# Splitting weight pieces by two recipes in turn, with the float32 words of all thirds in one place

## The chip, the cores and the metric

The kernel runs on one core of a Trainium2 chip. Its engines are TensorE (PE; its weight loads are shown as PEld), VectorE (DVE), ScalarE (ACT), GpSimd (POOL) and SyncE (SP), which here only issues transfers. The metric is the device time of one execution in microseconds (us); the median of the runs is quoted.

## The reference

Two layers are computed, one after the other, in float32: attention with a compressive memory, and a gated feed-forward layer.

```
# q, k, v: (4, 8, 576, 64); M_prev: (4, 8, 64, 64); z_prev: (4, 8, 64)
scores = q @ k^T / 8, causal;  a = softmax(scores);  local = a @ v
q_p = where(q > 0, q, exp(q) - 1) + 1
mem_out = (q_p @ M_prev) / (q_p @ z_prev + 1e-6)
x = sigmoid(beta) * mem_out + (1 - sigmoid(beta)) * local      # rows: 4*576 = 2304, columns: 8*64 = 512
xn = x / sqrt(mean(x*x) + 1e-6) * rms_g
out = (silu(xn @ w_gate) * (xn @ w_val)) @ w_out               # 512 -> 1536 -> 512
```

The three weight matrices arrive as float64; the host only lays inputs out.

## The kernel before

**Split numbers.** All matrix work runs on pairs of float16 numbers: a float32 operand, scaled by a power of two, is written as hi (its float16 rounding) and lo (what is left, in float16 too), and a product takes three matmuls: hi by hi, hi by lo, lo by hi. Most work of the other engines is making such pairs.

**Blocks.** The 2304 rows are 18 blocks of 128 (four batches of 576 rows, two batches taken together, so that each pair has eight full blocks and one block of two tails). For a block `q_stats`, `prep_q`, `phi_calc`, `prep_phi`, `prep_k` and `prep_v` split the rows of q, phi(q), k and v (tiles `row16`, shown as row; v in `v16`); transposing DMAs on SP's queue make qT, phT and kT of them (`tposed`; the first two blocks use TensorE and evictions by ACT instead). For one or more heads at a time, `u_scores` computes scores (tile sc) and moves them out with the mask on VectorE (L449, tile S), `u_exp` takes the exponential and the hi cast on ACT (L495, L497, tile P16), `u_lo` the lo on VectorE or POOL (L506) with a transposing DMA into PT, and `u_pv` multiplies by v (tile loc). `loc_evac` (L595, L601, L605), `x_norm` and `x_split` make the split x, its transposed form being xT, one for two blocks (a chunk of 256 rows; nine chunks).

**The feed-forward layer.** The 1536 inner columns are twelve groups of 128. For chunk c and group f, F = 12c + f: `m_proj` makes 24 matmuls (L762) into gv (gate and value), `m_act` the tanh on ACT (L768) and two operations on VectorE (L769, L772), `m_split` the hi on ACT (L793) and the lo on POOL (L794), `m_down` six matmuls by w_out (L816 to L818). PSUM has two gv buffers.

**The weights.** Gate and value weights come in 24 pieces of 128 x 512, numbered p = 8t + 4m + cc: t is the third of the inner columns, m is 0 for gate and 1 for value, cc the 128 rows of the model dimension. w_out has 12 pieces. For each piece:

- `load_w`: a 512 KB load of the float64 words into one of five raw places (`RING`), which is free again when the piece five earlier is converted. The first five are issued on SP's queue, the others on ACT's.
- `w_conv`: `f64_to_f32` makes float32 words of it with one operation on ACT (L687) and two on VectorE (L691 on the raw words, L692 on the result); `gram` adds their squares up on TensorE (csum, L135).
- `gv_scales(t)`, when all eight pieces of a third are there: reduction (L707), scale factors, and at the end `rgs` (L714), the scale of each piece's rows.
- `w_split`: the words become hi and lo in `wgv16`.

`wgv` is one tile of 25 places of 128 x 512 float32. The words of piece p lie in place p + 1; the pair hi, lo of piece p fills place p (`wgv16` is the same tile seen as float16). So hi of piece p overwrites the words of piece p - 1, and must wait until these have been read. `load_pre` borrows eight places of the last third (17 to 24) for early k and v rows, which only `first_gram` reads.

`wo` has the same scheme for w_out (words of piece f in place f + 1, its pair in place f), and its free places serve as raw ring and for other early data.

**`split` and its recipes.** `SPLIT` names the recipe, one string per third and one for w_out; `way_of` takes its characters in turn by the piece's number.

- "0": ACT writes hi from the words with the scale (L82), VectorE writes lo = words x scale - hi (L85).
- "1": ACT scales the words in place (L97), ACT casts hi (L101), POOL writes lo = words - hi (L104).
- "3": VectorE scales the words in place (L99), ACT casts hi (L101), POOL writes lo (L104).

**What sets the order.** The program is written as attention steps interleaved with feed-forward steps by a budget (`run`, `a_until`), the first blocks with a high priority; a scheduler then fixes each engine's order from the dependencies and these priorities before the run. On the chip each engine executes its list in that order, and an instruction that waits holds up all behind it on its engine.

Of the kernel before, what the change touches and what calls it, by code (L numbers as in the profile page):

```python
# [31 lines left out]
A3 = 0.2  # L32
A4 = 0.3
C2 = 8
SPLIT = ("3", "3", "3", "3")
VWAY = "11"
RING = 5
PACE = 5
# [7 lines left out]
def attn_memory_moe_kernel(  # L46
# [18 lines left out]
    NI = S // P  # L65
    TR = S - NI * P
    NC = DM // P
# [21 lines left out]
    def split(dst_hi, dst_lo, src, scale, way="0"):  # L89


        if way == "0":
            hi_cast(dst_hi, src, scale)
            lo_cast(dst_lo, src, scale, dst_hi)
            return
        if way in "12":
            nc.scalar.activation(src, src, AF.Copy, scale=scale)  # L97
        else:
            nc.vector.tensor_scalar(src, src, scale, None, op0=ALU.mult)  # L99
        if way in "135":  # L100
            nc.scalar.copy(dst_hi, src)  # L101
        else:
            nc.vector.tensor_copy(dst_hi, src)
        nc.gpsimd.tensor_tensor(dst_lo, src, dst_hi, ALU.subtract)  # L104
# [23 lines left out]
    def gram(acc, src, first, last):  # L128

        hi = src.bitcast(BF16).rearrange("p (f w) -> p f w", w=2)[:, :, 1]
        for g in range(4):
            w = hi[:, g * P : (g + 1) * P]
            nc.tensor.matmul(acc[:, :P], w, w, start=first and g == 0, stop=last and g == 3)  # L135

    csum = {}
# [24 lines left out]
    wgv = const.tile([P, 2 * NC * NT3 + 1, 512], F32, name="wgv")  # L162
# [73 lines left out]

    def load_pre(n):

        at = 1 + 4 * NC + 2 * (n - NI)
        pre[n] = wgv[:, at : at + 2, :]  # L240
        nc.sync.dma_start(out=pre[n], in_=qkv[n, :, :2, :])

# [390 lines left out]
    def piece(m, cc, t):  # L633
        return t * 2 * NC + m * NC + cc

    raws = {}
    NR = RING

# [7 lines left out]
    def after(ins, before, why):  # L646
        tc.add_manual_dep(
            ins.ins, before.ins.name,
            mybir.DependencyInfo(mybir.DependencyClass.Sync, mybir.DependencyReason.SCHED_ONLY),
            reason=why,  # L650
        )
# [7 lines left out]
    def load_w(m, cc, t):  # L659
        w = (w_gate, w_val)[m]  # L660
        p = piece(m, cc, t)
        raws[p] = hold(p, 2 * (p % NR))
        ins = (nc.sync if p < PACE else nc.scalar).dma_start(
            out=raws[p].bitcast(I64), in_=w[cc * P : (cc + 1) * P, t * 512 : (t + 1) * 512]
        )
        paced(ins, p)
# [12 lines left out]
    def f64_to_f32(raw, dst, p):  # L679

        r = raw.rearrange("p (f w) -> p f w", w=2)
        ri, di = r.bitcast(I32), dst.bitcast(I32)
        begun[p] = nc.scalar.activation(dst, r[:, :, 1], AF.Prelu, scale=2.0 ** -112, alpha=2.0 ** 32)  # L687
        if 2 * NC <= p < 6 * NC:

            after(begun[p], xdone[p // (2 * NC) - 1], "first blocks")  # L690
        nc.vector.tensor_scalar(ri[:, :, 0], ri[:, :, 0], 29, None, op0=ALU.logical_shift_right)  # L691
        nc.vector.scalar_tensor_tensor(  # L692
            out=di, in0=di, scalar=3, in1=ri[:, :, 0], op0=ALU.logical_shift_left, op1=ALU.bitwise_or
        )

    def way_of(table, third, i):
        return table[third][i % len(table[third])]
# [38 lines left out]

    def w_split(m, cc, t):
        p = piece(m, cc, t)
        src = wgv[:, p + 1, :]
        sc = rgs[:, t, m, cc : cc + 1]  # L740
        split(wgv16[:, p, :512], wgv16[:, p, 512:], src, sc, way_of(SPLIT, t, p % (2 * NC)))

    def wo_split(f):
        src = wo[:, f + 1, :]
        split(wo16[:, f, :512], wo16[:, f, 512:], src, wos[:, f // 4 : f // 4 + 1], way_of(SPLIT, NT3, f))

# [170 lines left out]
    for n in range(NI, 2 * NI):  # L917
        load_pre(n)
# [18 lines left out]
    for s in range(len(units) + LAG + 2):  # L937
        if s < len(units):
            n, h = units[s]
# [25 lines left out]
        if s < len(units):  # L965
            n, h = units[s]
# [8 lines left out]
    def w_conv(i):  # L975
        m, cc, t = pcs[i]
        p = piece(m, cc, t)
        f64_to_f32(raws.pop(p), wgv[:, 1 + p, :], i)
        held.pop(p)
        if cc == m == 0:  # L980
            csum[t] = ps.tile([P, 2, P], F32, tag="out", name="csum")
        gram(csum[t][:, m], wgv[:, 1 + p, :], cc == m == 0, cc == NC - 1 and m == 1)
        if i + PACE < len(pcs):
            load_w(*pcs[i + PACE])

# [52 lines left out]
    def conv(t):  # L1038
        return [lambda i=i: w_conv(i) for i, x in enumerate(pcs) if x[2] == t]

    def spl(t):
        return [lambda: gv_scales(t)] + [lambda x=x: w_split(*x) for x in pcs if x[2] == t]
# [96 lines left out]
```

## Time and profile before

| | |
|---|---|
| runs | 685.72, 685.72, 687.58 us; median 685.72 |
| profiled execution | 687.62 us, of which the span of its instructions is 685.9 |
| TensorE busy | 597.1 us (87% of the span), 6292 matmuls |
| VectorE busy | 480.8 us (70%) |
| ACT busy | 406.9 us (59%) |
| POOL busy | 232.3 us (34%) |
| mean granted TensorE clock | 0.938 of full speed |

The profile divides the span into 40 slices of 17 us. TensorE's busy share is 20 to 80% up to about 180 us and 90% or more in nearly all slices after that; the granted clock is at full speed from about 200 us on and lower in several slices before. VectorE is at 70% or more in every slice from 34 to 154 us. An idle stretch of an engine is shown with the engine or transfer that ended it (its releaser); an operation's duration includes the time in which it is held up after its start.

### The profile page before, as it was taken

How to read it: one execution, taken by the hardware profiler on the slowest of the kernel's cores; microseconds unless marked ns; L12 is line 12 of the kernel's file. 1: busy time of each engine (PE TensorE's matmuls, PEld its weight loads, DVE VectorE, ACT ScalarE, POOL GpSimd, SP SyncE). 2: the span in 40 equal slices, each digit the busy share in tenths (PEclk: the TensorE clock that was granted, in tenths of full speed). 3: DMA queues.
4: the chain of work that ended last, by engine and by line, in shares of the span. 5: the costliest groups of instructions: out<-in, count | busy, mean ns of one | idle time of the engine just before them, and what ended most of it. 6: DMA issues, size and time to landing. Idle time of an engine off the chain costs nothing.

```text
span 685.9 us, 16422 instructions
## 1 busy us (share of the span) xinstructions
PE 597.1 (87%) x6292; PEld 461.3 (67%) x6292; DVE 480.8 (70%) x1441; ACT 406.9 (59%) x845; POOL 232.3 (34%) x308
## 2 busy tenths in 40 slices
PE   2664367866899999999899999999999999999997
PEld 1553245745665587778678777767777878887774
DVE  3689997985685766679687776786887686873221
ACT  5788655665647676657556657766666464442322
POOL 1306544674467434323025231431322222212111
PEclk9985567977899999999999999999999999999999
DMA  8952589833935968844675865376664554441001
GB/s 271 411 148 83 188 272 227 184 77 80 176 69 89 191 126 166 166 88 88 118 155 123 167 131 113 64 137 142 123 131 103 107 78 93 80 76 34 32 1 31
DMA packets 186383, 88.13 MB, mean 128 GB/s; under 512 B 171712, under 2 KB 171712, under 8 KB 186304
## 3 DMA queue, kind: packets, MB, share of 16 engines
q1 hardware_dynamic: 181392, 70.81, 49.5%
q10 hardware_dynamic: 4912, 16.28, 7.1%
q8 instruction: 49, 0.80, 0.5%
q14 instruction: 30, 0.25, 0.1%
HBM read 36.20 MB, written 4.72 MB: 60 GB/s over the span
## 4 chain that ended last, share of the span: by engine, by line
PE 43%; DVE 17%; DMA 16%; ACT 13%; issue 5%; POOL 4%; SPq 1%; ACTq 0%; DVEq 0%; POOLq 0%
PE gv L762 23%; DMA kv<-in_qkv_dram 6%; DMA PT<-P 5%; PE out L816 4%; PE out L817 4%; PE out L818 4%; DVE S L449 3%; ACT junk L220 2%; PE sc L443 2%; DMA qT<-row 2%; ACT P L497 2%; PE sc L469 2%; ACT S L495 2%; DVE P L506 2%; DMA phT<-row 2%
## 5 line engine op out<-in xcount | busy, mean ns | idle before, releaser
L762 PE MATMUL gv<-xT,wgv 128*128 128x256 f16 x2592 | 363.4, 279 | 11.7 <-DVE th L772 6.4
L762 PEld LDWEIGHTS <-wgv 128*128 128x128 f16 x2592 | 253.2, 100 | 56.0 <-issue 7.6
L794 POOL TENSOR_TENSOR h<-th,h 128x256 f16<-128x256 f32 x96 | 71.5, 745 | 259.3 <-ACT h L793 201.2
L495 ACT ACTIVATE S<-S,nm 128x128 f32<-128x128 f32 (+4 forms) x144 | 80.2, 586 | 57.3 <-DVE nm L456 42.2
L443 PE MATMUL sc<-kT,qT 128*128 128x128 f16 x640 | 94.9, 224 | 12.9 <-DMA kT<-row 4.1
L506 DVE TENSOR_TENSOR P<-S,P 128x512 f16<-128x512 f32 (+2 forms) x80 | 61.0, 763 | 40.4 <-ACT P L497 39.7
L769 DVE SCALAR_TENSOR_TENSOR th<-th,gv 128x256 f32<-128x256 f32 x108 | 44.9, 416 | 61.0 <-ACT th L768 60.6
L768 ACT ACTIVATE th<-gv,wt 128x256 f32<-128x256 f32 x108 | 50.4, 467 | 59.4 <-PE gv L762 56.2
L449 DVE CUSTOM_DVE_ANT_0 S<-sc,mask,qsc 128x128 f32<-128x128 f32 (+3 forms) x128 | 66.6, 545 | 12.6 <-PE sc L443 12.0
L817 PE MATMUL out<-wo,h 128*128 128x512 f16 x192 | 72.8, 379 | 0.0
L816 PE MATMUL out<-wo,h 128*128 128x512 f16 x192 | 72.6, 379 | 0.1
L818 PE MATMUL out<-wo,h 128*128 128x512 f16 x192 | 71.8, 379 | 0.0
L443 PEld LDWEIGHTS <-qT 128*128 128x128 f16 x640 | 56.6, 100 | 21.9 <-issue 8.0
L497 ACT CAST P<-S 128x512 f16<-128x512 f32 (+2 forms) x104 | 62.2, 599 | 10.2 <-DMA PT<-P 9.0
L793 ACT CAST h<-th 128x256 f16<-128x256 f32 x96 | 38.5, 402 | 44.7 <-DVE th L772 44.2
L530 PE MATMUL loc<-v,PT 128*128 128x65 f16 x320 | 55.4, 197 | 5.7 <-DMA PT<-P 5.3
L532 PE MATMUL loc<-v,PT 128*128 128x65 f16 x320 | 54.9, 197 | 2.0 <-ACT PT L347 2.0
L531 PE MATMUL loc<-v,PT 128*128 128x64 f16 x320 | 54.9, 197 | 0.0
L772 DVE SCALAR_TENSOR_TENSOR th<-th,wt,gv 128x256 f32<-128x256 f32 x108 | 51.6, 478 | 1.9
L605 POOL TENSOR_TENSOR t<-t,t 128x256 f32<-128x256 f32 x36 | 31.4, 873 | 60.0 <-DVE t L601 57.7
L530 PEld LDWEIGHTS <-PT 128*128 128x128 f16 x320 | 31.6, 100 | 14.2 <-DMA PT<-P 10.8
L104 POOL TENSOR_TENSOR wgv<-wgv 128x512 f16<-128x512 f32 x24 | 31.7, 1321 | 26.8 <-ACT wgv L101 26.6
(222 smaller groups left out, 1104.4 us busy)
## 6 DMA issues: line engine op xcount, KB each, us to landing
kv<-in_qkv_dram SPq DMA_DIRECT2D x18, 512.0 KB, 4.8
wo<-in_moe_w_val_dram ACTq DMA_DIRECT2D x11, 512.0 KB, 4.7
q<-in_qkv_dram SPq DMA_DIRECT2D x18, 256.0 KB, 3.5
wo<-in_moe_w_gate_dram ACTq DMA_DIRECT2D x8, 512.0 KB, 6.0
wo<-in_moe_w_out_dram ACTq DMA_DIRECT2D x8, 512.0 KB, 5.1
qT<-qT SPq DMA_DIRECT2D x32, 128.0 KB, 2.6
out_dram<-res SPq DMA_DIRECT2D x16, 256.0 KB, 2.3
wo<-in_moe_w_gate_dram SPq DMA_DIRECT2D x4, 512.0 KB, 6.5
```

Source lines behind the costliest of these rows:

```text
L443: nc.tensor.matmul(t[:, g * w + j * P : g * w + (j + 1) * P], qT[n][:, t2, h, :], kT[blk_of[(b, j)]][:, h, :], start=(t2 == 0), stop=(t2 = ...
L449: nc.vector.tensor_tensor_reduce(out=s[:, g * w : (g + 1) * w], in0=t[:, g * w : (g + 1) * w], in1=mask[:, m0 : m0 + w], scale=qsc[n][:, 5:6],
L495: nc.scalar.activation(v_, v_, AF.Exp, bias=nm[:, g : g + 1], scale=-1.0)
L497: nc.scalar.copy(p16[:, : G * w], s[:, : G * w])
L506: eng.tensor_tensor(p16[:, w : 2 * w], s[:, :w], p16[:, :w], ALU.subtract)
L530: nc.tensor.matmul(a, phi_, vhi, start=(j == 0), stop=False)
L531: nc.tensor.matmul(a[:, :D], phi_, vlo, start=False, stop=False)
L762: nc.tensor.matmul(o, lhs, xT[c][:, rhs, :], start=(cnt == 0), stop=(cnt == 3 * NC - 1))
L794: nc.gpsimd.tensor_tensor(h16[:, 1], th, h16[:, 0], ALU.subtract)
L816: nc.tensor.matmul(o, hh, whi, start=(f == 0), stop=False)
L817: nc.tensor.matmul(o, hh, wlo, start=False, stop=False)
L818: nc.tensor.matmul(o, hl, whi, start=False, stop=(f == NF - 1))
```

## The change

`SPLIT` is "01" in all four entries: of each third, and of w_out, the pieces with an even number are split by recipe 0 (hi on ACT, lo on VectorE), those with an odd number by recipe 1 (two operations on ACT, lo on POOL). The words of piece p now lie in place 17 + p mod 8 for all three thirds, and `load_pre` borrows places 9 to 16. So the words of a third overwrite those of the third before, whose split must have read them; the pairs of the first two thirds no longer overwrite words. In the last third, words and pairs lie as before.

```
-SPLIT = ("3", "3", "3", "3")
+SPLIT = ("01", "01", "01", "01")
...
     def load_pre(n):
-        at = 1 + 4 * NC + 2 * (n - NI)
+        at = 1 + 2 * NC + 2 * (n - NI)
...
+    def words_at(p):
+        return 1 + 4 * NC + p % (2 * NC)
...
     def w_split(m, cc, t):
         p = piece(m, cc, t)
-        src = wgv[:, p + 1, :]
+        src = wgv[:, words_at(p), :]
...
     def w_conv(i):
-        f64_to_f32(raws.pop(p), wgv[:, 1 + p, :], i)
+        f64_to_f32(raws.pop(p), wgv[:, words_at(p), :], i)
-        gram(csum[t][:, m], wgv[:, 1 + p, :], cc == m == 0, cc == NC - 1 and m == 1)
+        gram(csum[t][:, m], wgv[:, words_at(p), :], cc == m == 0, cc == NC - 1 and m == 1)
```

NC is 4 and NI is 4. Because of four added lines, lines from 636 on have numbers higher by four in the changed kernel (L687 becomes L691, L663 becomes L667, L676 becomes L680, L768 becomes L772, L692 becomes L696).

The scheduler's order changes with it. On ACT, around the split of the first third, before the change (x is the split x of block 0, kv the rows of v being scaled, xT evictions and v casts follow):

```order
L82 ACTIVATE x_713<-t_0_580,xs 128x512
L101 CAST wgv<-wgv 128x512
L97 ACTIVATE kv_117<-kv_117,cb_92 128x512
L97 ACTIVATE kv_119<-kv_119,cb_92 128x512
L97 ACTIVATE kv_921<-kv_921,cb_92 128x512
L97 ACTIVATE kv_501<-kv_501,cb_92 128x512
L687 ACTIVATE wgv<-wo 128x512 x5
L347 CAST xT_716<-tp 128x4x128
```

and after it, from the same instruction on (the two operations on wgv stand there four times in turn, for the eight pieces; L691 is the word conversion):

```order
L82 ACTIVATE wgv<-wgv,rgs 128x512
L97 ACTIVATE wgv<-wgv,rgs 128x512
...
L97 ACTIVATE kv_117<-kv_117,cb_92 128x512
L97 ACTIVATE kv_119<-kv_119,cb_92 128x512
L97 ACTIVATE kv_917<-kv_917,cb_92 128x512
L97 ACTIVATE kv_501<-kv_501,cb_92 128x512
L82 ACTIVATE x_711<-t_0_580,xs 128x512
L101 CAST wgv<-wgv 128x512
L97 ACTIVATE kv_125<-kv_125,tcb_898 128x512
L101 CAST wgv<-wgv 128x512 x3
L101 CAST v_2_1089<-kv_117 128x8x64
```

The x cast has moved behind the split, and the five conversions of the middle third behind both.

On VectorE at the same place, before the change (fl and t belong to the attention output, ratio, kT and v to a rescaling of the first blocks):

```order
L99 TENSOR_SCALAR wgv<-wgv,rgs 128x512 x5
L291 TENSOR_TENSOR ratio<-cb_92,wo 128x4
L598 RECIPROCAL fl<-fl 128x4
L85 SCALAR_TENSOR_TENSOR x_713<-t_0_580,xs,x_713 128x512
L721 TENSOR_SCALAR wt<-wt 128x1
L302 TENSOR_SCALAR kT_192<-kT_192,ratio 128x1024
L304 TENSOR_SCALAR v_0_268<-v_0_268,ratio 128x1040
L302 TENSOR_SCALAR kT_473<-kT_473,ratio 128x1024
L601 TENSOR_TENSOR t_1_792<-loc_0_779,fl 128x256
L692 SCALAR_TENSOR_TENSOR wgv<-wgv,wo 128x512 x5
```

and after it:

```order
L291 TENSOR_TENSOR ratio<-cb_92,wo 128x4
L598 RECIPROCAL fl<-fl 128x4
L725 TENSOR_SCALAR wt<-wt 128x1
L85 SCALAR_TENSOR_TENSOR wgv<-wgv,rgs 128x512
L302 TENSOR_SCALAR kT_192<-kT_192,ratio 128x1024
L304 TENSOR_SCALAR v_0_268<-v_0_268,ratio 128x1040
L302 TENSOR_SCALAR kT_473<-kT_473,ratio 128x1024
L601 TENSOR_TENSOR t_1_788<-loc_0_775,fl 128x256
L85 SCALAR_TENSOR_TENSOR wgv<-wgv,rgs 128x512 x3
L85 SCALAR_TENSOR_TENSOR x_711<-t_0_580,xs,x_711 128x512
L696 SCALAR_TENSOR_TENSOR wgv<-wgv,wo 128x512 x5
```

Eight scalings are gone (three more stand just ahead of the first list), four lo's have come, and the lo of x stands behind them.

On ACT some 40 us later, before the change from the gate tanh of F = 1 (gv_984) on, with the first loads of w_out:

```order
L768 ACTIVATE th<-gv_984,wt 128x256
L101 CAST wgv<-wgv 128x512
L676 DMA wo<-in_moe_w_out_dram 128x512
L676 DMA rawo_1815<-in_moe_w_out_dram 128x512
L97 ACTIVATE kv_1101<-kv_1101,cb_92 128x512
L395 ACTIVATE ph<-q_1099 128x512
```

and after it, at the first loads of w_out (row_1172 and row_1305 are the rows of q and k of block 3, gv_1074 is F = 2):

```order
L82 ACTIVATE row_1172<-q_1094,qsc 128x8x64
L691 ACTIVATE wgv<-wo 128x512
L667 DMA wo<-in_moe_w_val_dram 128x512
L82 ACTIVATE row_1305<-kv_119,cb_92 128x8x64
L797 CAST h16k<-th 128x256
L691 ACTIVATE wgv<-wo 128x512
L772 ACTIVATE th<-gv_1074,wt 128x256
L691 ACTIVATE wgv<-wo 128x512
L667 DMA wo<-in_moe_w_val_dram 128x512
L680 DMA wo<-in_moe_w_out_dram 128x512 x2
```

The loads of w_out have moved behind loads and conversions of the last third's value pieces, and behind the rows of block 3.

## Rows read from the trace of the kernel before

**Rows 1.** Stretches of the span: length, busy us of each engine, clock, DMA, GB/s.
```profile
55.50:151.00 95.50, 59.09 (x536) 45.45 (x536) 87.92 (x228) 62.15 (x121) 55.60 (x51) 0.69 0.69 182
...
180.00:686.00 506.00, 488.81 (x5287) 378.54 (x5285) 340.79 (x1017) 290.17 (x607) 151.70 (x205) 1.00 0.53 106
...
200.00:236.00 36.00, 32.64 (x307) 20.74 (x306) 22.85 (x74) 25.60 (x54) 23.75 (x27) 1.00 0.64 119
```
**Rows 2.** Groups by line, 55.5 to 151 us: count, busy us, mean ns, idle before.
```profile
L104 POOL TENSOR_TENSOR wgv<-wgv 128x512 f16<-128x512 f32 x20 | 27.1, 1354 | 24.7 <-ACT wgv L101 24.5
...
L99 DVE TENSOR_SCALAR wgv<-wgv,rgs 128x512 f32<-128x512 f32 x24 | 14.1, 640 | 0.0
L691 DVE TENSOR_SCALAR wo<-wo 128x512 int32<-128x512 int32 x19 | 13.5, 723 | 1.3 <-DMA wo<-in_moe_w_val_dram 1.3
L101 ACT CAST wgv<-wgv 128x512 f16<-128x512 f32 x21 | 12.9, 614 | 5.3 <-POOL wgv L104 5.3
```
**Rows 3.** Single lines over the whole span: ns min/median/max, first and last start.
```profile
L99 DVE TENSOR_SCALAR wgv<-wgv,rgs x24: 452/476/1382, 55.5 to 139.7; 128x512 f32<-128x512 f32 x24
...
L691 DVE TENSOR_SCALAR wo<-wo x32: 405/421/1381, 13.4 to 123.8; 128x512 int32<-128x512 int32 x32
...
L85 DVE SCALAR_TENSOR_TENSOR row<-q,qsc,row x18: 740/752/1647, 25.2 to 527.0; 128x512 f16<-128x512 f32 x18
...
L85 DVE SCALAR_TENSOR_TENSOR row<-kv,cb,row x14: 735/744/752, 91.6 to 522.1; 128x512 f16<-128x512 f32 x14
```
**Rows 4.** Whom VectorE waited for, 55.5 to 151 us: total, times, longest.
```profile
DVE row L85 <- ACT row L82: 4.1, 1, 4.1
```
**Rows 5.** Transfers of phT, 80 to 115 us and whole run: count, us to landing.
```profile
phT<-row SPq DMA_TRANSPOSE x1, 10.9
...
phT<-row SPq DMA_TRANSPOSE x16, 2.8
```
**Rows 6.** ACT in order of time: start, us, line, operation, count, idle before.
```profile
55.99 0.72 ACT L82 ACTIVATE x<-t,xs 128x512 f16<-128x512 f32 x1 [1.02 <-POOL xs L618]
...
57.12 2.56 ACT L97 ACTIVATE kv<-kv,cb 128x512 f32<-128x512 f32 x4
59.59 2.88 ACT L687 ACTIVATE wgv<-wo 128x512 f32<-128x512 f32 x5
...
63.27 0.33 ACTq L663 DMA_DIRECT2D wo<-in_moe_w_val_dram  x1
...
97.41 0.33 ACTq L676 DMA_DIRECT2D wo<-in_moe_w_out_dram  x1
...
109.65 0.72 ACT L82 ACTIVATE row<-q,qsc 128x512 f16<-128x512 f32 x1 [5.51 <-DMA phT<-row]
```
**Rows 7.** VectorE in order of time, columns as in rows 6.
```profile
55.12 0.22 DVE L714 TENSOR_SCALAR rgs<-rg,wt 128x4 f32<-128x4 f32 x1
...
66.98 0.61 DVE L691 TENSOR_SCALAR wo<-wo 128x512 int32<-128x512 int32 x1 [1.34 <-DMA wo<-in_moe_w_val_dram]
...
72.43 0.15 DVE L595 SCALAR_TENSOR_TENSOR fl<-loc,wo 128x4 f32<-128x4 f32 x1
...
80.71 0.74 DVE L85 SCALAR_TENSOR_TENSOR x<-t,xs,x 128x512 f16<-128x512 f32 x1
...
90.00 1.65 DVE L85 SCALAR_TENSOR_TENSOR row<-q,qsc,row 128x512 f16<-128x512 f32 x1
...
99.23 0.42 DVE L707 TENSOR_REDUCE wmx<-csum 128x2 f32<-128x256 f32 x1
...
132.63 0.77 DVE L714 TENSOR_SCALAR rgs<-rg,wt 128x4 f32<-128x4 f32 x2
```
**Rows 8.** POOL and TensorE in order of time; ACT's waits in 136 to 162 us.
```profile
89.61 1.49 POOL L104 TENSOR_TENSOR wgv<-wgv 128x512 f16<-128x512 f32 x1 [3.37 <-ACT wgv L101]
...
163.74 6.37 PE L762 MATMUL gv<-xT,wgv 128*128 128x256 f16 x44 [2.22 <-DVE th L772]
...
ACT wgv L101 <- POOL wgv L104: 4.6, 3, 2.6
```

## The prediction

> **What bounds the kernel now.** I read the stages first [rows 1]. From 180 us to the end TensorE is busy for 488.8 of 506.0 us at full clock: there the end is set by how much matrix work is left, and only an earlier arrival at that state saves time. Before it TensorE mostly starves: in 55.5 to 151.0 it is busy 59.1 of 95.5 us at a mean granted clock of 0.69, a mixture of 1.2 and 2.4 GHz. In the same stretch VectorE is busy 87.9 of 95.5 us, ACT 62.2 and POOL 55.6. VectorE therefore bounds 55.5 to 151, the stretch in which all 24 VectorE scalings of gate and val pieces and 20 of the 24 POOL subtracts lie [rows 2]. Of its 7.6 idle us, 4.1 are one wait for ACT [rows 4], which itself waits 5.51 us for the transposing DMA of phT [rows 6]. From 151 to 164 the bound is a chain: TensorE waits for the last third's splits and for the gate arithmetic behind them, and goes on at 163.74 [rows 8]. The wo pieces lie in 200 to 236, where TensorE is busy 32.6 of 36.0 us, so their edits are nearly covered.
>
> **Against which time.** The profiled execution took 687.62 us (span 685.9 plus 1.7 around it); the median of the three runs is 685.72, 1.9 lower. I sum differences against the profiled one and set them off from the median.
>
> **The change, part by part.** Prices of the added operations stand in rows of the same shapes: a scaled hi cast on ACT 0.72 us, a scaling in place on ACT 0.64 (four took 2.56) [rows 6], a lo on VectorE 0.744 [rows 3].
>
> *VectorE's work, -5.2.* All 24 scalings go, 14.1 us of VectorE time in the bound stretch [rows 2]. Every second piece gets a lo on VectorE: 12 x 0.744 = 8.9 us. Net -5.2. Bounds: the scalings' mean is 640 ns [rows 2] against a median of 476 [rows 3], so they are stretched there by 1.34; if the new lo's are stretched as much, they cost 12.0 and the net is -2.1. The kv rows (735 to 752 ns) show none of it, so I take -5.2. The Trainium skill (SBUF — State Buffer, Who interferes with whom) says that a VectorE instruction with two SBUF inputs contends with a GpSimd instruction that reads SBUF, which is the form of the new lo; the q rows, 740 to 1647 ns, agree that it can happen [rows 3]. By that rule alone the term would be the -2.1.
>
> *POOL out of VectorE's way, -3.* Ten of the 20 subtracts in the stretch go, of 1.354 us mean: 13.5 of POOL's 55.6 busy us, 24%. Other VectorE operations are stretched there: L691 has a mean of 723 [rows 2] against a median of 421 [rows 3], 19 x 0.30 = 5.7 us. A quarter of it would be 1.4; L692 and the small operations next to it are stretched too, and the first third's subtracts now fall into VectorE's new idle time (next part), so I take -3, between bounds of 0 and -5.7.
>
> *The words' new wait, +9.5.* The words of a third now lie where those of the third before lay, so L687 (and VectorE's L692 behind it) of a piece waits for the split of its predecessor. In the new order eight split operations and four kv scalings stand on ACT ahead of the hi cast of the first x block, and four casts, one kv scaling and two v casts ahead of the first L687 that follows. Walked with rows: the scales are ready at 55.3, the end of the second L714 [rows 7], and ACT is free; eight operations at 0.64 end at 60.4, the kv scalings at 63.0, where the x cast starts instead of at 55.99; seven casts and scalings at 0.55 to 0.64 put L687 at 67.6 instead of 59.59 [rows 6]. VectorE has its four lo's done at about 60.7, waits until 63.7 for the x cast (3.0), does its part, waits from 64.4 to 68.3 for the first words (3.9) and loses 1.0 to two xT evictions between words on ACT. The load of the next raw piece, issued at 63.27 [rows 6] and used at 66.98 after 1.34 of idle [rows 7], is now issued at about 71.5 and lands at 75.1 after 2.9 of idle, 1.6 more. Together 9.5 us of new VectorE idle. Queued behind it: the attention output of block 1 (L595 at 72.43 [rows 7]), which comes at about 78, and with it block 1's x. Not all of it reaches TensorE: the first third's weights are split at 69 instead of 91.1 (the eighth subtract, at 89.61 [rows 8]), so the first projections need not wait for them. Bounds: 6, if the load is off the path and the x cast's wait is half filled, and 9.5. I take 9.5, as each of its waits has a row.
>
> The same wait holds the last third's words behind the middle third's splits. Before, its sums were reduced at 99.23 and its scales written from 132.63 on [rows 7]: 33 us of slack cover the delay, so it costs nothing; without that cover it would cost what eight conversions take one after the other, about 5 us (L687 five at 2.88 [rows 6]).
>
> *The phT collision, -4.1.* The phT transpose took 10.9 us to land in 80 to 115 us, where its median over the run is 2.8 [rows 5]; four w_out loads are issued right around it, the first at 97.41 [rows 6]. In the new order ACT issues w_out loads only after gv2's tanh, behind the rows of q3 and kv3, so this transpose should run free. Bounds: 0 (the val loads that now stand there do the same) and -8.1. I take VectorE's own idle, -4.1 [rows 4].
>
> *The last third's chain, -2.4.* In 136 to 162 ACT's hi casts wait 4.6 us for the subtracts [rows 8], since hi of a piece overwrites the words of the piece before it. That stays in the last third, but four of the eight links now go through a VectorE lo, 0.74 instead of 1.35 us [rows 2, 3]: 4 x 0.61 = 2.4. Bounds 0 and -4.6.
>
> *ACT's added work, 0.* 36 pieces: 18 scalings at 0.64 and 18 hi casts dearer by 0.72 - 0.614 [rows 2] make +13.4 us. Beyond the first third (costed above), ACT's idle time takes it: it is busy 62.2 of 95.5 us. A rule speaks against the change: the Trainium skill (ScalarE: Activation LUTs, Rules for kernel authors) says to multiply on VectorE, not on ScalarE. The rows agree on the size, 0.48 there and 0.64 here, but VectorE is the engine without room. By the rule the swap of 18 scalings alone would be a loss of 2.9 us.
>
> *The wo pieces, 0.* VectorE and POOL lose work, ACT gains it; TensorE is idle for 3.4 us in 200 to 236, so the bounds are -3.4 and, with ACT late by six scalings, +3.8.
>
> *After 164, 0.* In the new order the row of q4 stands behind the tanh of gv11 and three v casts, so block 4 gains only some 2 us; but more projection matmuls stand ahead of its scores and fill TensorE.
>
> Sum: -5.2 - 3 + 9.5 - 4.1 - 2.4 = -5.2: 682.4 for a profiled run, **680.5** for the median.
>
> **Rivals.** *Slower: the late words decide.* Mechanism: ACT's eight split operations ahead of the x cast, at 55 to 75 us. It decides if block 1's x split (VectorE, 80.71 before [rows 7]) comes later than 84: then +9.5 stands against -5.2 or -2.1 alone, and with the collision still there the time is 685.7 + 4.3 to 7.4 = 690 to 693. For it: VectorE idles where it was full. Against it: the first third's weights come 20 us earlier, and much of VectorE's work in 82 to 90 now stands behind q2's row.
> *No difference.* If TensorE has only attention of block 4 to do when its projections run out, the lead of 5 shrinks to the 2 of q4's row and less: 684 to 687. For it: q4's new place; against it: TensorE's 97% from 180 on. That the change doesn't relieve VectorE (stretched lo's, chain as long as before) ends here too: -2.1 - 3 + 9.5 - 4.1 = +0.3.
> *Much faster.* The collision goes whole (-8.1), POOL's stretch too (-5.7), the new wait costs 6 and the chain gives 4.6: -5.2 - 5.7 + 6 - 8.1 - 4.6 = -17.6. Half way between that and the forecast: 674.
>
> **How the numbers follow.** A measurement of this kernel can tell about 0.3%, 2.1 us. Forecast (2.1 to 9 faster) 0.44; much faster 0.14; within 2.1 us 0.17; slower 0.25. So faster 0.58, same 0.17, slower 0.25. The range reaches from 672 (some 0.06 below it) to 690.5 (some 0.12 above it).
>
> **What would show it.** In the changed profile: VectorE's idle between 60 and 76 us near 9; the middle third's first word conversion near 67.6; q2's row earlier than 90.0 [rows 7]; phT landing in about 3 us; the last third's scales written before 129; TensorE above 95% some 5 us earlier. I am wrong if the second x block's split comes after 84, if the new lo's mean is near 1 us, or if TensorE's idle after 180 grows by as much as it fell before.

## The result and the profile after

The changed kernel took 693.6 us (median of four runs, 693.11 to 697.04) against 686.65 for the kernel before beside it: a ratio of 1.0112, 95% interval 1.0073 to 1.015. By the ratio it is 7.7 us slower (7.0 by the medians), where 5 us faster was forecast, and above the range. Ratios leave out executions that lie over 1.5% above the fastest of the same kernel, so differences taken from ratios are not quite those of the medians. The profiled execution, the slowest of the four, took 697.04 us with a span of 695.0, so the profile has 9.1 us more span to explain.

The stretches of [rows 1] in the changed kernel, and a new one, 115 to 145 us. Columns: length, busy us of PE, PEld, DVE, ACT and POOL, granted clock, DMA share, GB/s.

```profile
55.50:151.00 95.50, 52.48 (x504) 41.68 (x501) 70.26 (x207) 64.64 (x125) 33.96 (x38) 0.75 0.74 166
115.00:145.00 30.00, 21.03 (x209) 17.47 (x208) 21.34 (x69) 18.60 (x38) 10.99 (x11) 0.79 1.13 215
180.00:695.00 515.00, 491.58 (x5334) 381.43 (x5331) 346.85 (x1024) 296.29 (x617) 144.99 (x200) 1.00 0.54 108
200.00:236.00 36.00, 31.87 (x333) 21.27 (x332) 23.33 (x68) 27.32 (x54) 17.28 (x21) 1.00 0.60 88
```

The same 115 to 145 us in the kernel before:

```profile
115.00:145.00 30.00, 23.70 (x270) 20.14 (x269) 29.85 (x92) 19.35 (x40) 18.21 (x17) 0.90 0.69 163
```

VectorE is relieved as intended: 70.3 busy us in 55.5 to 151 instead of 87.9, and 21.3 of 30 us instead of 29.9 in 115 to 145. TensorE does not gain by it; it is busy for 52.5 us instead of 59.1 and so has matrix work left over. From 180 us on it idles for 23.4 us instead of 17.2. The column that rose is the DMA share: 1.13 instead of 0.69. The view adds up the time that packets took, so a share above 1 means that packets stood on an engine beside one another.

**Where the time goes.** Up to about 97 us the changed kernel goes as the prediction walked it, and is then ahead. VectorE, in order of time (start, duration, engine, line, operation, tiles; in brackets the idle time before it and what ended it):

```profile
64.12 0.75 DVE L85 SCALAR_TENSOR_TENSOR x<-t,xs,x 128x512 f16<-128x512 f32 x1 [2.25 <-ACT x L82]
68.40 5.63 DVE L696 SCALAR_TENSOR_TENSOR wgv<-wgv,wo 128x512 int32<-128x512 int32 x5 [3.53 <-ACT wgv L691]
...
78.01 0.15 DVE L595 SCALAR_TENSOR_TENSOR fl<-loc,wo 128x4 f32<-128x4 f32 x1
...
84.70 0.75 DVE L85 SCALAR_TENSOR_TENSOR x<-t,xs,x 128x512 f16<-128x512 f32 x1
...
87.75 0.74 DVE L85 SCALAR_TENSOR_TENSOR row<-q,qsc,row 128x512 f16<-128x512 f32 x1
95.50 0.75 DVE L85 SCALAR_TENSOR_TENSOR row<-ph,qsc,row 128x512 f16<-128x512 f32 x1 [0.47 <-ACT row L82]
...
115.97 0.75 DVE L85 SCALAR_TENSOR_TENSOR row<-ph,qsc,row 128x512 f16<-128x512 f32 x1 [4.57 <-ACT row L82]
```

Block 1's x comes at 84.70 instead of 80.71, but the row of q2 at 87.75 instead of 90.00 [rows 7]. Then ACT, the first w_out load, and the ones that matter later:

```profile
63.38 0.70 ACT L82 ACTIVATE x<-t,xs 128x512 f16<-128x512 f32 x1
67.71 1.76 ACT L691 ACTIVATE wgv<-wo 128x512 f32<-128x512 f32 x3
...
105.20 0.79 ACTq L680 DMA_DIRECT2D wo<-in_moe_w_out_dram  x1
...
115.22 0.72 ACT L82 ACTIVATE row<-ph,qsc 128x512 f16<-128x512 f32 x1 [6.11 <-DMA qT<-row]
...
125.21 0.40 ACTq L680 DMA_DIRECT2D wo<-in_moe_w_out_dram  x1
129.08 0.34 ACTq L680 DMA_DIRECT2D wo<-in_moe_w_out_dram  x1
132.70 0.33 ACTq L680 DMA_DIRECT2D wo<-in_moe_w_out_dram  x1
...
173.48 0.71 ACT L82 ACTIVATE x<-t,xs 128x512 f16<-128x512 f32 x1
```

Before, the w_out loads began at 85.3 us. Now they begin at 105.2, since the last val conversions wait for the middle third's splits, and three of them are issued from 125 on, while SyncE issues kT and PT of block 3. What the transfers issued in 123 to 146 us took in the changed kernel (tile, issuing queue, operation, count, size, median us from issue to landing):

```profile
wo<-in_moe_w_out_dram ACTq DMA_DIRECT2D x4, 512.0 KB, 13.0
PT<-P SPq DMA_TRANSPOSE x3, 11.3
kT<-row SPq DMA_TRANSPOSE x1, 14.4
```

and in the kernel before:

```profile
rawo<-in_moe_w_out_dram ACTq DMA_DIRECT2D x3, 512.0 KB, 4.2
PT<-P SPq DMA_TRANSPOSE x5, 4.1
kT<-row SPq DMA_TRANSPOSE x1, 5.1
```

These transfers look to be in each other's way. The queues' shares of the 16 engines in that stretch (packets, MB, share; q1 carries the transposes, which SyncE issues, q10 the loads, which ACT issues):

```profile
q1 hardware_dynamic: 5280, 1.31, 60.3%
q10 hardware_dynamic: 736, 2.62, 50.6%
```

Together that is 111%. In the kernel before, the same stretch has half of that:

```profile
q1 hardware_dynamic: 6567, 1.62, 38.5%
q10 hardware_dynamic: 300, 1.10, 17.4%
```

The Trainium skill (DMA: Bandwidth & Descriptors, Queues, rings and completion order) says that SP and ACT have a queue each on the same 16 engines, and that an engine takes turns between its queues packet by packet; the rows agree in that both sorts of transfer slow down alike, loads from 4.2 to 13.0 us and PT from 4.1 to 11.3. The waits that follow, TensorE first, then VectorE:

```profile
139.15 1.44 PE L443 MATMUL sc<-kT,qT 128*128 128x128 f16 x12 [5.18 <-DMA kT<-row]
```

```profile
138.92 0.43 DVE L695 TENSOR_SCALAR wo<-wo 128x512 int32<-128x512 int32 x1 [4.89 <-DMA wo<-in_moe_w_out_dram]
...
165.63 0.43 DVE L695 TENSOR_SCALAR rawo<-rawo 128x512 int32<-128x512 int32 x1 [3.90 <-DMA rawo<-in_moe_w_out_dram]
...
180.44 1.23 DVE L85 SCALAR_TENSOR_TENSOR row<-q,qsc,row 128x512 f16<-128x512 f32 x1
```

VectorE takes its instructions in order, so all of block 3's work behind the two conversions waits too. ACT casts block 3's x at 173.48 instead of 163.08; q4's row follows at 180.44 instead of 166.79. The kernel before has one such crowd of transfers, at 97 to 113 us (phT, 10.9 us [rows 5]). The changed one has two: qT at 106 to 115 us (9.4 us, the 6.11 us wait of ACT above), and this one.

### The profile page after: what moved, and what is told of

Its sections match the earlier page's. It is cut to its first block, busy times and chain, and to the rows that moved or that the text cites. A ratio compares the mean times of both kernels' runs of the same rounds, so it can differ in the third digit from the quotient of the medians.

```text
span 695.0 us, 16407 instructions
## 1 busy us (share of the span) xinstructions
PE 591.3 (85%) x6292; PEld 459.0 (66%) x6292; DVE 471.9 (68%) x1423; ACT 417.4 (60%) x863; POOL 204.6 (29%) x290
## 4 chain that ended last, share of the span: by engine, by line
PE 49%; DMA 18%; ACT 13%; DVE 11%; issue 6%; POOL 2%; SPq 1%; ACTq 0%; POOLq 0%; DVEq 0%
PE gv L766 26%; DMA PT<-P 5%; DMA kv<-in_qkv_dram 5%; PE out L820 4%; PE out L821 4%; PE out L822 4%; DMA qT<-row 3%; PE sc L443 2%; DMA wo<-in_moe_w_out_dram 2%; DVE S L449 2%; ACT junk L220 2%; DMA wo<-in_moe_w_val_dram 2%; PE sc L469 2%; ACT P L497 2%; ACT S L495 1%
## 5 line engine op out<-in xcount | busy, mean ns | idle before, releaser
L766 PEld LDWEIGHTS <-wgv 128*128 128x128 f16 x2592 | 251.8, 100 | 59.5 <-issue 12.9
L495 ACT ACTIVATE S<-S,nm 128x128 f32<-128x128 f32 (+4 forms) x144 | 80.2, 584 | 55.8 <-DVE nm L456 39.6
L773 DVE SCALAR_TENSOR_TENSOR th<-th,gv 128x256 f32<-128x256 f32 x108 | 44.9, 416 | 61.4 <-ACT th L772 60.9
L772 ACT ACTIVATE th<-gv,wt 128x256 f32<-128x256 f32 x108 | 50.1, 465 | 59.8 <-PE gv L766 57.5
L449 DVE CUSTOM_DVE_ANT_0 S<-sc,mask,qsc 128x128 f32<-128x128 f32 (+3 forms) x128 | 66.7, 545 | 12.5 <-PE sc L443 10.9
L605 POOL TENSOR_TENSOR t<-t,t 128x256 f32<-128x256 f32 x36 | 29.1, 808 | 61.4 <-DVE t L601 57.3
L506 POOL TENSOR_TENSOR P<-S,P 128x512 f16<-128x512 f32 (+1 forms) x24 | 27.3, 1136 | 50.6 <-ACT P L497 40.2
```

What stands on the lines that cost most here:

```text
L449: nc.vector.tensor_tensor_reduce(out=s[:, g * w : (g + 1) * w], in0=t[:, g * w : (g + 1) * w], in1=mask[:, m0 : m0 + w], scale=qsc[n][:, 5:6],
L495: nc.scalar.activation(v_, v_, AF.Exp, bias=nm[:, g : g + 1], scale=-1.0)
L506: eng.tensor_tensor(p16[:, w : 2 * w], s[:, :w], p16[:, :w], ALU.subtract)
L766: nc.tensor.matmul(o, lhs, xT[c][:, rhs, :], start=(cnt == 0), stop=(cnt == 3 * NC - 1))
```

## Experiments

Ratios are against the kernel before, run beside each kernel; the microseconds in the text are ratio differences times 686.65. The columns after the ratio are read from the profiled execution: issue of the first w_out load, DMA share in 115 to 145 us, cast of block 3's x on ACT, and span.

| run | words in | recipes | ratio (95%) | w_out from | DMA share | x of block 3 | span |
|---|---|---|---|---|---|---|---|
| before | own places | old | 1 | 85.3 | 0.69 | 163.1 | 685.9 |
| after | shared | new | 1.0112 (1.0073–1.015) | 105.2 | 1.13 | 173.5 | 695.0 |
| e1 | own | new | 0.9973 (0.9938–1.0009) | 86.3 | 0.76 | 159.0 | 679.4 |
| e2 | shared | old | 1.0266 (1.0221–1.0312) | 105.5 | 0.94 | 182.7 | 703.8 |
| e3 | middle third apart | new | 1.0045 (1.0012–1.0079) | 87.5 | 0.75 | 165.1 | 684.1 |
| e4 | shared, 7 light loads | new | 0.9922 (0.9889–0.9955) | 104.5 | 0.68 | 165.4 | 682.9 |
| e5 | own, 7 light loads | old | 0.9993 (0.9966–1.0021) | 86.1 | 0.61 | 161.9 | 686.2 |
| e6 | first third apart | new | 1.0000 (0.9967–1.0034) | 104.0 | 0.78 | 163.7 | 680.8 |
| e7 | own | new, w_out old | 0.9936 (0.9902–0.997) | 86.8 | – | – | – |
| e8 | own | new, first third old | 0.9912 (0.9879–0.9945) | 85.1 | 0.54 | 158.0 | 678.6 |
| e9 | own | new, both of these old | 0.9954 (0.9932–0.9977) | 83.8 | 0.65 | 157.0 | 681.2 |
| e10 | shared, 5, 7, 9 light | new | 1.0006 (0.998–1.0032) | 103.2 | 0.76 | 163.5 | 680.6 |
| e11 | own, 7 light loads | new | 1.0028 (1.0006–1.0049) | 86.9 | 0.47 | 167.2 | 685.8 |
| e12 | own | ACT and POOL only | 1.0107 (1.0076–1.0137) | 84.6 | 0.63 | 171.4 | 691.2 |
| e13 | shared, 5, 7, 9 held | new | 1.0054 (1.0027–1.0081) | 102.7 | 0.98 | 173.3 | 690.9 |
| e14 | shared, 2, 3, 4 light | new | 0.9985 (0.9956–1.0014) | 104.1 | 0.91 | 165.8 | 688.0 |
| e15 | shared | new, first third old | 1.0132 (1.0091–1.0174) | 105.6 | 1.00 | 176.6 | 693.2 |

The time of block 3's x goes with the span: the correlation over these 16 executions is 0.93, with 0.89 us of span for each microsecond. (e7's profiled execution took 689.87 us, 7.1 above its median of 682.8, and is left out.)

**The two halves of the change.** e1 keeps the new recipes and puts the words back; e2 keeps the new places and puts the recipe back:

```
e1:  words_at(p): return 1 + p            load_pre: at = 1 + 4 * NC + 2 * (n - NI)
e2:  SPLIT = ("3", "3", "3", "3")
```

> The recipes alone: every piece is split in turn by ACT and VectorE or by ACT and POOL, but its words stay in their old places (a third has its own). Theory 'places' (the 7 to 9 us come from the words' new wait and from the loads that it puts off): the new wait is gone and VectorE's relief stays, so 680 to 685 us against 686. Theory 'recipes' (the split operations that ACT now does, eight ahead of a block's work, are the loss): about 693, as the whole change.

> The places alone: the words of all thirds lie in the last third's place, but every piece is split as before (VectorE scales, ACT casts, POOL subtracts). Theory 'places': the words wait for the old, longer splits, so the whole loss or more, 693 to 700 us. Theory 'recipes': 685 to 688, as before.

The recipes alone gave a gain of 1.9 us that the interval does not separate from nothing; the places alone cost 18.3 us, with the old recipe, and 9.5 us on top of the new one (1.0112 to 0.9973). The loss belongs to the places; why the old recipe makes it larger was not tried. The crowd at 123 to 146 us can't be the whole of it: in e2, the slowest kernel of all, the transfers of that stretch land nearly as fast as in the kernel before (PT in 4.2 us, the loads in 4.8, and kT):

```profile
kT<-row SPq DMA_TRANSPOSE x1, 6.4
```

**Which third's wait.** e3 gives the middle third's words their own place, e6 the first third's:

```
e3:  return 1 + p if p >= 2 * NC else 1 + 4 * NC + p
e6:  return 1 + p if p < 2 * NC else 1 + 4 * NC + p % (2 * NC)
```

> The whole change, but the words of the middle third lie in a place of their own (slots 9 to 16, where the loaded blocks of the other batch lay until their sums were taken), so a third's words never wait for the split of the third just before. Theory 'places': the wait is gone; the first words of the middle third come at 60 to 63 us instead of 67.7, the w_out loads start before 100 instead of at 105, and the time is 680 to 686 us. Theory 'recipes': 692 to 695, as the whole change.

> The new recipes, with the first third's words in their old place, and the middle and last third's both in the last third's place: only the last third's words wait for a predecessor's splits. Theory 'last third' (the wait that was put at nothing holds the last third's conversions, and so the val and w_out loads, behind the middle third's splits): the first w_out load is issued after 103 us as in the changed kernel, and the time is 690 to 694. Theory 'middle third' (the wait ahead of the second x block, put at 9.5 us, is the loss): w_out still late or not, the time is 684 to 688, as with the recipes alone.

e6 went against the theory "last third", in its time: with the last third's wait alone, and with w_out as late as in the whole change (104.0 us), the loss is gone. The middle third's wait costs 7.7 us when it stands beside the last third's (1.0112 to 1.0000); without both (e3) 4.6 come back. So late loads alone are not the loss. e3 missed its forecast (680 to 686; its ratio stands for about 690). Nothing makes a third wait for the one just before there, and yet the first word of the middle third was converted at 67.06 us, not at 60 to 63: the order holds it there, not the shared place. e3 and e1 have the same recipes and neither wait, and still lie 4.9 us apart. In e6 the transfers issued in 115 to 131 us landed sooner, by the same view:

```profile
wo<-in_moe_w_out_dram ACTq DMA_DIRECT2D x5, 512.0 KB, 5.0
PT<-P SPq DMA_TRANSPOSE x3, 7.6
phT<-row SPq DMA_TRANSPOSE x1, 7.4
kT<-row SPq DMA_TRANSPOSE x1, 7.1
```

The queues' shares there are no lower than the changed kernel's 111%, so the share alone does not tell how long a transfer takes:

```profile
q1 hardware_dynamic: 5119, 1.50, 57.4%
q10 hardware_dynamic: 848, 3.08, 52.5%
```

e6 had issued four w_out loads by 112.0 us, the whole change two: there ACT stood until 115.2 for qT. Whether that decides was not tried.

**Is it the crowd of transfers?** In e4, e5 and e11 seven of the twelve w_out loads move an eighth of their columns, and the rest is not loaded; in e10 and e14 three do:

```
e4, e5, e11:  n = DM if f in (1, 6, 8, 10, 11) else 64
e10:          n = 64 if f in (5, 7, 9) else DM
e14:          n = 64 if f in (2, 3, 4) else DM
              dma_start(out=r.bitcast(I64)[:, :n], in_=w_out[f * P : (f + 1) * P, :n])
```

> The whole change, with an eighth of the columns loaded in seven of the twelve w_out loads (the rest of their words is what the slot held, so the output is not the reference's). Theory 'collision' (the loss comes when w_out loads land among the transposing DMAs of blocks 2 and 3 in 115 to 145 us, where kT took 14 us and VectorE waited 4.9 us for w_out): kT lands in 3 to 5 us and the time falls by 4 to 8 us, to 685 to 690. Theory 'order' (the loss is the later work of ACT and VectorE itself, whatever the loads weigh): within 2 us of 693.6.

> The kernel before, with the same seven w_out loads cut to an eighth of their columns (the output is not the reference's). Lightening them made the changed kernel 12.5 us faster. Theory 'collision' (the change moves w_out loads into the transposing DMAs of blocks 2 and 3, where before they did little harm): 684 to 688 us, so that with light loads the changed kernel is 3 to 6 us faster than this one. Theory 'both alike' (w_out loads cost either kernel the same): 673 to 678, with the changed kernel still 5 to 8 us behind.

> The recipes alone (old places), with the same seven w_out loads cut to an eighth (the output is not the reference's). Beside the changed kernel with light loads (681.1) it gives the price of the words' wait without the jam. The forecast put that wait at 9.5 us: then 671 to 674. If the wait costs nothing where no loads are jammed: 680 to 682. If loads jam in this order as well, something between by chance of the order: 675 to 679.

> The whole change, with only three of the twelve w_out loads cut to an eighth of their columns: those of pieces 5, 7 and 9, which were issued at 125.2, 129.1 and 132.7 us among kT and three PT of block 3 and landed after 12 to 14 us (the output is not the reference's). Theory 'jam at 124 to 146' (these three loads and four transposes share the DMA engines, and block 3 waits for them): most of the 12.5 us of the seven light loads come back, 681 to 686. Theory 'all loads' (the traffic of the whole stretch from 98 us on counts): less than half comes back, 688 to 692.

> Control to the run that cut pieces 5, 7 and 9: the whole change with the w_out loads of pieces 2, 3 and 4 cut to an eighth instead (the output is not the reference's). These were issued at 115.4 to 123.1 us and landed in 3.8 to 5.7. Theory 'jam at 124 to 146': the three later loads come a little earlier but are still there, so 690 to 694. Theory 'any lighter load or new order': 684 to 688 like pieces 5, 7 and 9.

Light loads take 13.0 us from the changed kernel and nothing measurable from the kernel before (0.5 us, interval across 1). With light loads the changed kernel is 7.3 us faster than the recipes alone (e4 against e11): without the traffic the words' wait shows no price. So the weight of the loads counts where they come late, and not where they come early. Three light loads were enough for 7.3 us (e10), with ACT's order that of the whole change up to the load at 125 us. Its transfers issued in 121 to 134 us:

```profile
wo<-in_moe_w_out_dram ACTq DMA_DIRECT2D x1, 512.0 KB, 6.4
wo<-in_moe_w_out_dram ACTq DMA_DIRECT2D x3, 64.0 KB, 4.0
PT<-P SPq DMA_TRANSPOSE x3, 6.2
kT<-row SPq DMA_TRANSPOSE x1, 7.6
```

kT lands in 7.6 us instead of 14.4, PT in 6.2 instead of 11.3. The control e14 did not stay at 690 to 694: cutting pieces 2, 3 and 4 gave 8.7 us, as its rival "any lighter load or new order" said. It is no clean control either. Its order is another one, and between 123 and 134 us ACT issues a single w_out load in it, a light one:

```profile
128.42 0.33 ACTq L680 DMA_DIRECT2D wo<-in_moe_w_out_dram  x1
134.19 0.34 ACTq L680 DMA_DIRECT2D wo<-in_moe_w_out_dram  x1
```

Two of the three full loads that were to stay beside kT came only at 134.19 and 135.21, when kT (issued at 126.56, 6.1 us to landing) had landed. So e14 goes against the theory as it was put, and does not separate a thinner crowd from a new order. e11 is a warning in the other direction: less to load, and 3.8 us slower than e1. The schedule is made anew for each kernel, and its chance is worth some 4 to 5 us either way (e11 and e1, e3 and e1).

**The same with the whole computation.** e13 holds three loads until block 3's keys have landed:

```
 moved[0] = nc.sync.dma_start_transpose(out=dst, in_=src)
 tposed(kT[n], flat(t), n); keys[n] = moved.get(0)
 paced(ins, len(pcs) + f); f in (5, 7, 9) and after(ins, keys[3], "keys first")
```

> The whole change, nothing left out, with one edit: the w_out loads of pieces 5, 7 and 9 are issued only after the transposing DMA of block 3's keys (kT) has landed. Theory 'jam': kT lands in under 9 us instead of 14.4, PT behind it in 3 to 8 instead of 13.6, and the time falls to 684 to 690 against 693.6. Theory 'order': the later loads only make the w_out conversions later: 692 to 698.

It gave 4.0 us (1.0112 to 1.0054), no more than the chance of an order, and less than the theory asked for (691.24 us, where 684 to 690 was expected). kT took 10.5 us instead of 14.4, where under 9 was expected; TensorE's wait on it fell from 5.18 to 1.8 us, and PT took 4.5 in the median. But block 3's x came no earlier (173.3). Who waited for whom in 100 to 175 us, TensorE (total us, times, longest):

```profile
PE gv L766 <- DVE th L776: 11.4, 2, 9.7
PE loc L530 <- DMA PT<-P: 6.5, 1, 6.5
PE csum L135 <- DVE wo L696: 5.3, 4, 1.8
```

The time gained did not come by way of block 3's x, so this run speaks for the crowd only in that kT and PT land sooner behind fewer loads.

**ACT ahead of the first x block.** The first third, the w_out pieces or both keep the old recipe:

```
e7:   SPLIT = ("01", "01", "01", "3")      own places
e8:   SPLIT = ("3", "01", "01", "01")      own places
e9:   SPLIT = ("3", "01", "01", "3")       own places
e15:  SPLIT = ("3", "01", "01", "01")      shared places
```

> The recipes alone (old places) for the 24 gate and val pieces; the 12 w_out pieces are split as before. If the new recipe of the w_out pieces costs nothing, as forecast, 687 to 689 like the recipes alone; if ACT's six more scalings and dearer casts there are late, 683 to 686; if VectorE's relief there was a gain, 690 to 692.

> The recipes alone (old places) from the middle third on; the first third is split as before, so that ACT goes to the first x block at 56 us and not after the split operations. Theory 'ACT ahead of the x cast': the recipes lose 3 to 6 us in 56 to 85 us, and this gives 681 to 685. Theory 'no harm there': 687 to 690, since VectorE's relief of the first third is gone.

> The recipes alone (old places), for the middle and the last third only; the first third and the w_out pieces are split as before. If the two gains add (the first third split as before gave 6.6 us on the recipes alone, the w_out pieces 5.1), 675 to 678 us; if both go back to the same idle time, 680 to 683; 686 if they cancel.

> The whole change with its places, but the first third's pieces are split as before (VectorE scales, ACT casts, POOL subtracts), so ACT's eight split operations no longer stand ahead of the first x block. Theory 'ACT ahead of the x cast': 5 us less than the whole change, 686 to 690. Theory 'jam': the middle third's words now wait for the longer old splits, the w_out loads come as late as before and meet kT and PT again, 692 to 697.

With own places, leaving the first third alone gains 4.2 us on the recipes (e8 against e1), and block 0's x is cast at 55.8 instead of 60.9 us. With shared places it gains nothing (1.0132 against 1.0112, intervals overlapping), although the split operations ahead of block 0's x are gone in e15 too (cast at 55.7): there TensorE waits longest for PT, whose transfers issued from 134.60 us on stand among w_out loads again (133.89 and 135.15):

```profile
PE loc L530 <- DMA PT<-P: 17.7, 4, 8.8
```

The w_out pieces' recipe changed sign between e7 (2.5 us gained by keeping the old one) and e9 (2.9 lost), so it is not settled and small.

**Is it VectorE's relief that pays?** In e12 no piece of the middle and last third is split by VectorE: SPLIT = ("3", "1", "1", "3") with own places.

> As the run that leaves the first third and the w_out pieces as before, but every piece of the middle and the last third is split by ACT and POOL (scaling and cast on ACT, subtract on POOL), none by VectorE. If VectorE's relief is what pays (5.9 us of lo casts less), 672 to 676 us; if ACT's and POOL's longer chain of three operations decides in the last third (136 to 162 us), 680 to 685.

VectorE has less to do than in e9, and the kernel is 10.5 us slower. POOL's subtracts in 100 to 185 us, e12:

```profile
L104 POOL TENSOR_TENSOR wgv<-wgv 128x512 f16<-128x512 f32 x15 | 19.4, 1291 | 15.8 <-ACT wgv L101 15.8
```

and e9:

```profile
L104 POOL TENSOR_TENSOR wgv<-wgv 128x512 f16<-128x512 f32 x7 | 9.4, 1338 | 4.6 <-ACT wgv L101 4.5
```

The wait of POOL on ACT's hi casts grew from 4.6 to 15.8 us, so the chain over ACT and POOL is likely the longer one, as its rival said (though slower than the 680 to 685 it gave). There is no crowd of transfers here (DMA share 0.63): block 3's x is late for another reason. Which of POOL's and ACT's operations decides was not tried.

## Why the prediction was wrong

Two steps failed. The terms that e1 tests (VectorE's work, POOL, the last third's chain) stood for a gain of 10.6 us and gave 1.9. The terms of the places (+9.5 and -4.1) stood for a loss of 5.4 us and gave 9.5: moving the w_out loads was counted as a gain, and they met the next transposes. Of the 12.9 us between the forecast and the result, 8.7 are the first step and 4.1 the second. The dividing line is not sharp, since the walk of the words' wait holds delays that belong to the recipes.

**The words' new wait, +9.5.** The walk held: x at 63.38 (63.0 forecast), the first word at 67.71 (67.6), L595 at 78.01 (78), and VectorE was idle for 6.7 of the 16 us from 60 to 76 (busy 9.28), where near 9 was forecast; the other 2.2 are in the five L696 at 68.40, 1.13 us each where single ones take 0.69. The places cost 9.5 us on top of the recipes (e1 against after). The equal number is a coincidence. The first word comes at 67.06 in e3 too, where the middle third has its own place, and at 63.6 in e1 and e6: what the walk priced is an order that one scheduling gave and another did not. And by 95.5 us the kernel was 2.5 us ahead again (the row of phi stands at 95.50 above, and before at 97.96, next fence), and light loads take the price away (e4, e11). The places acted, as far as the runs show, through the loads that they put off. VectorE before:

```profile
97.96 0.74 DVE L85 SCALAR_TENSOR_TENSOR row<-ph,qsc,row 128x512 f16<-128x512 f32 x1
```

**The last third's words, 0.** By itself nearly right: e6 against e1 is 1.9 us, within the intervals. But the text counted scales (slack of 33 us; the last third's came at 131.22, not before 129), and not the transfers that the last val conversions release. "Of a step that is moved every DMA counts" was not followed here: nobody walked the w_out loads from 85 to 105 us past block 3's transposes.

**The phT collision, −4.1, bounds 0 to −8.1.** This step failed. phT landed in 3.5 us, as forecast, and qT behind it in 9.4: the crowd met the next transpose, and VectorE's wait of 4.1 us behind phT came back as one of 4.57 behind qT (at 115.97). A second crowd at 123 to 146 us came on top. In place of a gain there was a loss, which light loads put at 7.3 us (e10) to 13.0 us (e4), each give or take the 4 to 5 us of a new order; the term's bounds left no room for a loss, because only one transpose was looked at.

**VectorE's work, −5.2, and POOL out of its way, −3.** The work went, the time did not. The rows of [rows 2] in after:

```profile
L104 POOL TENSOR_TENSOR wgv<-wgv 128x512 f16<-128x512 f32 x9 | 10.9, 1225 | 17.9 <-ACT wgv L101 17.9
```

```profile
L695 DVE TENSOR_SCALAR wo<-wo 128x512 int32<-128x512 int32 x19 | 9.6, 505 | 8.3 <-DMA wo<-in_moe_w_out_dram 5.6 <-DMA wo<-in_moe_w_val_dram 2.7
L85 DVE SCALAR_TENSOR_TENSOR wgv<-wgv,rgs 128x512 f16<-128x512 f32 x10 | 8.1, 830 | 1.5 <-ACT wgv L82 1.4
```

The new lo takes 830 ns in the mean, between the 744 taken and the stretched bound.

```profile
L85 DVE SCALAR_TENSOR_TENSOR wgv<-wgv,rgs x10: 739/752/1214, 57.1 to 148.9; 128x512 f16<-128x512 f32 x10
```

That row counts 55.5 to 151 us (ns min/median/max); the last two of the twelve follow at 156.76 and 160.84 (1.13 and 0.90 us). Four of the twelve took 0.90 us or more, and these are the ones that started while POOL ran an operation with two inputs in SBUF, as here (VectorE's, then POOL's):

```profile
148.86 1.11 DVE L85 SCALAR_TENSOR_TENSOR wgv<-wgv,rgs 128x512 f16<-128x512 f32 x1
148.26 1.16 POOL L506 TENSOR_TENSOR P<-S,P 128x512 f16<-128x512 f32 x1 [3.61 <-issue]
```

The other eight took 0.74 to 0.75; four of them, at 90.61 to 94.28, ran while POOL stood idle. The rule of the Trainium skill (SBUF — State Buffer, Who interferes with whom), that such instructions contend, agrees; the forecast's 744 ns was right for most because few met. The mean of L691 (now L695) fell from 723 to 505. Some 10 us of lo's replace scalings of 14.1. Yet the recipes alone gained 1.9 us where these two terms and the next stood for 10.6. Of the difference 4.2 us is the first third (e8), whose price the prediction had put into the words' wait. Most of the rest is not located: e8 shows 6.0 us as what the recipes can give here.

**The last third's chain, −2.4.** Not seen in after: from its scales (131.22) to its last cast (161.77) it took 30.5 us, before 25.7 (132.63 to 158.32). VectorE and ACT stood for w_out words in between. The stretch also took 26.6 us in e10, with the crowd thinned, 24.6 in e8 and 19.8 in e1, so it moves with the order by more than the term, and the term stays open.

**ACT 0, wo pieces 0, after 164 0.** The wo pieces' sign is open (e7, e9). After 164 the forecast was a gain of nothing; TensorE's idle time from 180 on grew by 6.2 us, and before 180 it did not fall either (80.3 us instead of 71.7). Block 1's x after 84 was named as proof against the prediction, and it came at 84.70. The rival "late words decide" had that place and 690 to 693 us, nearest to the truth of all; but e15, with no split operation of ACT ahead of block 0's x, is as slow, and block 1 was not what ended late.

**What stays open.** That the loss belongs to the places is shown by e1 and e2. That it runs through the late w_out loads is well supported for the changed kernel: lighter loads give 7.3 to 13.0 us with shared places (e10, e14, e4) and nothing clear with own places (0.5 us in e5, a loss of 3.8 in e11). That it is their crowd with kT and PT at 123 to 146 us is argued from the rows. It is not shown apart from the new order that each edit brings: e14 does not tell the two apart, e13 thinned the crowd without bringing x forward, in e6 late loads went by with a share as high, and e2 loses most while its transfers there land fast.

**A better kernel.** e8, own places and the new recipes from the middle third on, is 6.0 us faster than the kernel before (0.9912, interval 0.9879 to 0.9945), and so about 2% faster than the changed one.

## What to carry to other kernels

When a buffer is shared, ask what the instruction that now waits releases: the next load is issued behind it, and its new place among the other transfers can cost more than the wait itself. Where an engine is full, relief pays only if what stands next to it (the DMA engines, the chain over the other two engines) has room. An edit that makes a scheduler start over is worth several microseconds by its order alone, so test a cause with more than one edit and with a control.

## What the runs showed of the hardware

Transposing DMAs slow down far more than their size suggests. phT lands in 2.8 us in the median over the run [rows 5]; kT took 14.4 us with 512 KB loads in flight, and the loads 13.0 instead of 4.2, although the two queues moved only 3.9 MB in those 23 us. The transposes have half the loads' bytes there (1.31 against 2.62 MB) and more of the engines' time (60.3 against 50.6%).
